# A hint for ScalarE's branch, one output store on ScalarE's queue, and a fallback path whose transfers go to GpSimd's queue

## The chip, the core and the metric

The kernel runs on one core of a Trainium2 chip. A core has TensorE (matrix multiplications, PE in the profile, with its weight loads as PEld), VectorE (DVE), ScalarE (ACT), GpSimd (POOL) and SyncE (SP, which here only issues transfers). Each engine works through its own list of instructions; they wait for each other and for transfers on semaphores. The metric is the device time of one execution in microseconds; the time of a kernel is the median of several runs.

## What is computed

Two parts follow each other. The first is an attention over blocks: a small matrix P of 8 x 8 per batch and head is normalised five times by rows and columns (Sinkhorn), the blocks of k and v are mixed by P, and each of the 8 blocks of 96 queries attends to its own mixed block. The second is a gated layer with a spatial mixing over the 768 positions.

```python
P = sort_net                                # (4, 8, 8, 8)
for _ in range(5):
    P = exp(P - max(P, -1)); P = P / (sum(P, -1) + 1e-9); P = P / (sum(P, -2) + 1e-9)
k_sorted, v_sorted = P @ blocks(k), P @ blocks(v)
attn = softmax(scale * q_b @ k_sb.T)        # per block of 96
x = (attn @ v_sb) as (4, 768, 512)
h = relu(x @ w_in); u, v = halves of h      # 512 + 512
v_n = (v - mean) / sqrt(var + 1e-6)
gated = u * (w_spatial @ v_n + b_spatial)
out = gated @ w_out                         # (4, 768, 512), float32
```

## The kernel before

Inputs of the four batches are loaded in turn and everything stays in on-chip memory until the output. The order of the work is written out by hand in the string ORDER: each word is a unit with its arguments (`OJ:3:4:0:512` calls `u_OJ` for batch 3, tile 4, columns 0 to 512), and each unit appends its instructions to the lists of the engines that it names. Nothing reorders them, so the order of two stores on SP is the order of their words.

Loads of q, k, v and of the weights go through GpSimd's queue (`u_L`, lines 158 to 181). SP issues the first load of sort_net (line 184) and of q (line 343), the copies of mixed v into blocks (`u_VC`, line 418, 24 transfers), four transposing transfers (`u_XD`, line 501), and all stores of the output: `u_OS` (line 645) for two row tiles at once, and for the last batch also `u_OJ` (line 692) for one tile of 128 rows. ScalarE issues no transfer.

The end of the program is batch 3. TensorE multiplies the gated tiles with w_out (`u_OH`, line 680), ScalarE or VectorE copies the result from PSUM to SBUF (`u_OI`, through the helper lines 110 and 112), and SP stores it (`u_OJ`). The last words of ORDER are

```python
OH:1:3:4:0:512:0:4 OI:D:3:0:0:512 OI:D:3:5:256:512 OI:A:3:4:0:512 OJ:3:1:0:512 OJ:3:5:256:512 OJ:3:4:0:512
OJ:3:0:0:512
```

so the last copies are of tile 0 and of half of tile 5 by VectorE and of tile 4 by ScalarE, and the last four stores on SP are those of tile 1, of half of tile 5, of tile 4 and of tile 0.

The fast way through the attention skips the subtraction of maxima. Whether that was safe is found out while the kernel runs: `u_CK` and `u_CF` (lines 694 to 713) form a flag from the sums, and `u_LF` (line 715) loads it into a register on every engine. Behind the last word of ORDER stands an If (line 773): when the flag is above 0, `general_path` (line 724) computes everything again in a safe form. With the inputs given the flag is 0, so the path is skipped: each engine executes a branch over the path's instructions, some semaphore steps on the If's line, and the closing steps on line 800, where SP waits for all semaphores, all engines meet, and the semaphores are cleared.

`u_BH` (line 718) marks the place of a branch hint for TensorE and VectorE; in the trace the two hint instructions stand at 0.8 us, at the start of these engines' lists.

Of the kernel before, what the change touches and what calls it, by code (L numbers as in the profile page):

```python
# [45 lines left out]
SH:3:3:0:0 GH:D:3:0:0 SH:0:3:0:1 OS:2:2 SH:1:3:1:1 GH:P:3:1:1 SH:2:3:3:1 OH:3:3:2:0:512:0:4 GH:D:3:0:1 OS:2:0:0:1  # L46
OS:2:0:1:2 OH:1:3:3:0:512:0:4 GH:P:3:3:1 OI:A:3:2:0:512 OI:A:3:3:0:512 OJ:3:2:0:512 OH:2:3:5:0:256:0:4 OJ:3:3:0:512
OH:0:3:5:256:512:0:4 OI:D:3:5:0:256 OH:3:3:1:0:512:0:4 OH:2:3:0:0:512:0:4 OI:A:3:1:0:512 OJ:3:5:0:256
OH:1:3:4:0:512:0:4 OI:D:3:0:0:512 OI:D:3:5:256:512 OI:A:3:4:0:512 OJ:3:1:0:512 OJ:3:5:256:512 OJ:3:4:0:512
OJ:3:0:0:512  # L50
"""

# [13 lines left out]
def kernel(  # L66
# [12 lines left out]
    nc = tc.nc  # L79

    B, H, S, D = q.shape
# [8 lines left out]
    KC = DM // 128  # L90
    FC = DH // 128
    HP = H // 2
# [11 lines left out]

    def ps_tile(n, dt=FP32):
        return psum.tile([128, 2, 512 if dt == FP32 else 1024], dt, name=f"ps{n}", tag=f"ps{n}")

    def copy(eng, out, in_):
        if eng == "A":
            nc.scalar.copy(out=out, in_=in_)  # L110
        else:
            nc.vector.tensor_copy(out=out, in_=in_)
# [9 lines left out]
    p_all = const.tile([BH, NB, NB], FP32, name="p_all")  # L122
# [27 lines left out]
    st = {}  # L150
# [30 lines left out]
            nc.gpsimd.dma_start(out=w_out_sb, in_=moe_w_out.rearrange("(fc p) n -> p fc n", p=128))  # L181

    def load_sort_net():
        nc.sync.dma_start(out=p_all, in_=sort_net.rearrange("b h i j -> (b h) i j"))

    def u_S0():
        load_sort_net()
# [37 lines left out]
    def u_SK(n, safe=False):  # L225
        n = int(n)
        rows, cols = (first[:, 0:NB], first[:, NB:2 * NB]) if n == 0 else (rowsum, colsum)
        over_rows = lambda x: x.to_broadcast([BH, NB, NB])
        over_cols = lambda x: _raw_ap(x, 0, [x.ap[0], [0, NB], x.ap[1]])
        if safe:  # L230
            nc.vector.reduce_max(out=rowsum, in_=p_all, axis=AX.X)
            nc.vector.tensor_sub(out=p_all, in0=p_all, in1=over_rows(rowsum))
        nc.scalar.activation(out=p_all, in_=p_all, func=AF.Exp)
        nc.vector.reduce_sum(out=rows, in_=p_all, axis=AX.X)
        if safe:
            nc.vector.tensor_scalar_add(out=rows, in0=rows, scalar1=1e-9)
        nc.vector.reciprocal(out=rowsum, in_=rows)
        nc.vector.tensor_mul(out=p_all, in0=p_all, in1=over_rows(rowsum))
        nc.vector.reduce_sum(out=cols, in_=p_all.rearrange("p i j -> p j i"), axis=AX.X)
        if safe:  # L240
            nc.vector.tensor_scalar_add(out=cols, in0=cols, scalar1=1e-9)
        nc.vector.reciprocal(out=colsum, in_=cols)
        to = p16.rearrange("p (i j) -> p i j", i=NB) if n == 4 else p_all
        nc.vector.tensor_mul(out=to, in0=p_all, in1=over_cols(colsum))
        if n == 4:
            nc.vector.transpose(out=p_t, in_=p16)

    def u_PR(ps):
        pr = ps_tile(ps)[:, 0, 0:NB * BH].rearrange("p (i y) -> p i y", i=NB)
        for i in range(NB):  # L250
            nc.tensor.matmul(
                pr[:, i, :], lhsT=spread[:, (i % NI) * NB:(i % NI + 1) * NB].rearrange("p j t -> p (j t)"),
                rhs=p_t[:, (i // NI) * BH:(i // NI + 1) * BH], start=True, stop=True,
            )
        st["pr"] = pr
# [6 lines left out]
    def u_P0(lo, hi):  # L262
        lo, hi = int(lo), int(hi)
        n, pr = hi - lo, st["pr"]
        nc.vector.tensor_mul(
            out=pd(0)[:, lo:hi].rearrange("p h (i t) -> p h i t", t=TB),
            in0=_raw_ap(mask16, 0, [mask16.ap[0], [0, n], [0, NB], [1, TB]]),
            in1=_raw_ap(pr, lo, [pr.ap[0], [1, n], [BH, NB], [0, TB]]),
        )

    def u_PC(eng):
        copy(eng, prep_sb, st["pr"])

    def u_PD(b, lo, hi):
        b, lo, hi = int(b), int(lo), int(hi)
        n = hi - lo
        nc.gpsimd.tensor_mul(
            out=pd(b)[:, lo:hi].rearrange("p h (i t) -> p h i t", t=TB),
            in0=_raw_ap(mask16, 0, [mask16.ap[0], [0, n], [0, NB], [1, TB]]),
            in1=_raw_ap(prep_sb, b * H + lo, [prep_sb.ap[0], [1, n], [BH, NB], [0, TB]]),  # L280
        )
# [103 lines left out]
    def u_KT(ps, eng, b, hp):  # L385
        mixed("k", "kT", ps, eng, int(b), int(hp))
# [14 lines left out]
    def u_VM(ps, eng, b, hp):  # L401
        b, hp = int(b), int(hp)
        t = ps_tile(ps)
        for hh in range(2):
            nc.tensor.matmul(
                t[:, hh, 0:G * D], lhsT=pd(b)[:, 2 * hp + hh, :], rhs=st["v", b][:, 2 * hp + hh, :],
                start=True, stop=True,
            )
        copy(
            eng,  # L410
            vm[:, :, 2 * hp:2 * hp + 2, 0:D].rearrange("p g h d -> p h g d"),
            t[:, :, 0:G * D].rearrange("p h (g d) -> p h g d", g=G),
        )

    def u_VC(b, lo, hi):
        b = int(b)
        for i in range(int(lo), int(hi)):
            nc.sync.dma_start(
                out=vb[b % 2][:, i].rearrange("c h d -> c (h d)"),
                in_=vm[i * TB:(i + 1) * TB].rearrange("t g h d -> t g (h d)"),  # L420
            )
# [75 lines left out]
    def u_XD(b, ih, lo=0, hi=4):  # L497
        b, ih, lo, hi = int(b), int(ih), int(lo), int(hi)
        if ("xT", b) not in st:
            st["xT", b] = att.tile([128, 2, KC, HW], BF16, name="xT", tag="xT", bufs=2)  # L500
        nc.sync.dma_start_transpose(
            out=st["xT", b][:, ih, lo:hi].rearrange("p k (i c) -> p (k i) c", i=NI),
            in_=st["x", b, ih][:, lo:hi].rearrange("p k i c -> p (k i c)"),
        )

    def u_XT(ps, eng, b, ih, lo):
        b, ih, lo = int(b), int(ih), int(lo)
        if ("xT", b) not in st:
            st["xT", b] = att.tile([128, 2, KC, HW], BF16, name="xT", tag="xT", bufs=2)
        t = ps_tile(ps, BF16)[:, 0, 0:2 * HW].rearrange("p (k i c) -> p k i c", k=2, i=NI)  # L510
        for k in range(2):
            for i in range(NI):
                nc.tensor.transpose(t[:, k, i, :], st["x", b, ih][:, lo + k, i, :], ident[0:BLK, 0:BLK])
        copy(eng, st["xT", b][:, ih, lo:lo + 2].rearrange("p k (i c) -> p k i c", i=NI), t)
# [125 lines left out]
            st["o", b, n0] = ld.tile([128, 3, DM], FP32, name="o_sb", tag="ld")[:, 0:2]  # L640
        copy(eng, st["o", b, n0][:, lo:hi], st["o_ps", b, n0][:, lo:hi])

    def u_OS(b, n0, lo=0, hi=2):
        b, n0, lo, hi = int(b), int(n0), int(lo), int(hi)
        nc.sync.dma_start(
            out=out[b].rearrange("(c p) n -> p c n", p=128)[:, n0 + lo:n0 + hi, :],
            in_=st["o", b, n0][:, lo:hi],
        )
# [38 lines left out]
        st["o1", b, n, c0] = ld.tile([128, 3, DM], FP32, name="o1_sb", tag="ld")[:, 0, 0:c1 - c0]  # L687
        copy(eng, st["o1", b, n, c0], st["o1_ps", b, n, c0])

    def u_OJ(b, n, c0, c1):  # L690
        b, n, c0, c1 = (int(x) for x in (b, n, c0, c1))
        nc.sync.dma_start(out=out[b, n * 128:(n + 1) * 128, c0:c1], in_=st["o1", b, n, c0])

    def u_CK():
        nc.vector.memset(bad, 0.0)
# [21 lines left out]

    def u_BH():
        tc.mark_branch_hint_location(
            "general", hint="LikelyTaken", engines=[mybir.EngineType.PE, mybir.EngineType.DVE])  # L720

    units = {name[2:]: f for name, f in locals().items() if name.startswith("u_")}

    def general_path():


        st.clear()
        load_sort_net()
        for n in range(5):
            u_SK(n, safe=True)  # L730
        u_PR(0)
        u_P0(0, 8)
        u_PC("A")
        for b in range(B):
            if b > 0:
                u_PD(b, 0, 8)
            for x in ("q", "k", "v"):
                u_L(x, b, 0, H)
            for hp in range(HP):
                u_VM(2, "A", b, hp)  # L740
            u_VC(b, 0, NB)
            for hp in range(HP):
                u_QN(2, "A", b, hp)
                u_KT(3, "D", b, hp)
                for ih in range(2):
                    u_SM(b, hp, ih)
                    u_AT(2, b, hp, ih)
            for ih in range(2):
                u_XD(b, ih, 0, HP)
            for n in range(0, G, 2):  # L750
                u_VP(n % 4, "A", b, n, n + 1)
                u_ST(b, n)
                u_ST(b, n + 1)
            u_LN(b, 0, G)
            for n in range(G):
                u_LA(b, n)
            for m in range(2):
                for ih in range(2):
                    u_UP(2 * m + ih, "A", b, m, ih)
            for mc in range(FC):  # L760
                u_SP(mc, b, mc)
                u_GT("D", b, mc)
            for n in range(0, G, 2):
                u_OP(n % 4, b, n)
                u_OE("A", b, n)
                u_OS(b, n)
# [38 lines left out]
```

## Time and profile before

| what | value |
|---|---|
| median of 3 runs | 161.39 us (161.30 to 161.57) |
| time of the profiled execution | 161.53 us |
| its span, first to last instruction | 159.7 us |
| granted TensorE clock | 0.996 |
| instructions | 3977 |
| read from HBM / written | 24.78 MB / 6.29 MB |
| line 692 (`u_OJ`), issues on SP | 7, median 333 ns each, 149.8 to 155.4 us |
| line 692, from issue to landing | 2.0 / 2.4 / 2.7 us (lowest, median, highest) |
| GpSimd's last transfer counters on line 773 | 508 ns, at 150.8 us |
| GpSimd's drain on line 800 | 1461 ns, at 151.3 us |

The profile is one execution. A page gives each engine's busy time, the span in 40 slices (a digit is the busy share of the slice in tenths), the transfer queues, the chain of work that ended last, and the costliest groups of instructions. Beside the page there are views of the same trace: the timeline, the instructions of one source line, the waits, and the transfers in a window. A row of a source line has the line, the engine (a q behind its name means its instruction queue: branches, semaphores, transfer issues), the operation, the count, the durations in ns (lowest, median, highest) and the times of the first and last start in us. The time of a run is 1.8 us longer than the span.

### The profile page before, as it was taken

The page shows a single profiled execution, that of the slowest core. Times are in us where ns is not written, and L with a number is a line of the kernel's source. Part 1 is how long each engine was busy: PE and PEld are TensorE (multiplying, and loading weights), DVE is VectorE, ACT ScalarE, POOL GpSimd, SP SyncE. Part 2 cuts the span into 40 slices and gives each one's busy share as a digit, 9 for nine tenths or more (in the row PEclk, how much of TensorE's full clock was granted, in tenths as well). Part 3 has the DMA queues.
Part 4 walks back from the last instruction along what each step waited for, and adds up shares of the span by engine and source line. Part 5 has one row for each costly group of instructions (what it writes and reads, how often), then busy time and mean ns, then how long its engine had stood idle before and what let it go on. Part 6 is the DMA issues. An engine that isn't in the chain of part 4 may idle for free. (4 is left out here: it accounts for less than half of the span.)

```text
span 159.7 us, 3977 instructions
## 1 busy us (share of the span) xinstructions
PE 147.6 (92%) x1647; PEld 89.2 (56%) x1661; DVE 113.1 (71%) x261; ACT 85.7 (54%) x117; POOL 42.2 (26%) x46
## 2 busy tenths in 40 slices
PE   6997989999999999999999999999999999899840
PEld 2355867845686668556465654655655554455410
DVE  4786889638995679867838669897558956947620
ACT  3556799968889409478572446555432242340220
POOL 7942782292000034040000650210004440005300
PEclk9999999999999999999999999999999999999998
DMA  3999999999999999950000657300911377037253
GB/s 84 259 204 204 204 208 202 208 224 239 269 207 202 204 226 241 214 92 4 0 4 0 123 90 131 61 4 0 290 71 34 69 259 266 0 137 259 96 202 112
DMA packets 27526, 23.58 MB, mean 148 GB/s; under 512 B 7280, under 2 KB 24432, under 8 KB 27504
## 3 DMA queue, kind: packets, MB, share of 16 engines
q0 software_dynamic: 14352, 11.80, 46.6%
q1 hardware_dynamic: 13152, 11.49, 25.1%
q8 instruction: 14, 0.23, 0.6%
q14 instruction: 8, 0.07, 0.2%
HBM read 24.78 MB, written 6.29 MB: 195 GB/s over the span
## 5 line engine op out<-in xcount | busy, mean ns | idle before, releaser
L620 POOL TENSOR_TENSOR gt<-z,u_sb 128x768 bf16<-128x768 f32 x10 | 16.4, 1642 | 76.1 <-DVE rec_all L490 55.1
L442 ACT ACTIVATE ex<-ps 96x768 bf16<-96x768 f32 x32 | 24.4, 804 | 7.9 <-PE ps L437 7.8
L604 PE MATMUL ps<-wspT,v_sb 128*128 128x384 bf16 x144 | 25.4, 326 | 0.0
L592 PE MATMUL ps<-xT,w_in_sb 128*128 128x384 bf16 x128 | 23.3, 326 | 0.6 <-ACT o_sb L110 0.6
L491 DVE TENSOR_TENSOR x_sb<-ps,rec_all 96x512 bf16<-96x512 f32 x32 | 22.0, 687 | 1.1
L549 PE MATMUL ps<-w_in_sb,xT 128*128 128x512 bf16 x88 | 21.6, 379 | 0.5 <-issue 0.2
L566 DVE BATCH_NORM_STATS2 stats<-v_sb 128x6 f32<-128x512 bf16 x24 | 16.3, 680 | 5.5 <-ACT v_sb L116 4.3
L610 DVE TENSOR_TENSOR z<-ps,b_bc 128x768 f32<-128x768 f32 x12 | 11.5, 956 | 11.2 <-PE ps L604 11.2
L604 PEld LDWEIGHTS <-v_sb 128*128 128x128 bf16 x144 | 13.3, 98 | 8.4
L116 ACT ACTIVATE u_sb<-ps 128x768 bf16<-128x768 f32 x15 | 12.2, 812 | 10.8 <-PE ps L592 7.9
L116 ACT ACTIVATE v_sb<-ps 128x1024 bf16<-128x1024 f32 (+1 forms) x10 | 9.8, 982 | 14.4 <-PE ps L549 14.4
L592 PEld LDWEIGHTS <-w_in_sb 128*128 128x128 bf16 x128 | 11.8, 98 | 8.7 <-issue 0.9
L630 PE MATMUL ps<-w_out_sb,gt 128*128 128x512 bf16 x68 | 16.3, 379 | 0.2
L110 ACT COPY o_sb<-ps 128x1024 f32<-128x1024 f32 (+1 forms) x10 | 8.4, 839 | 14.7 <-PE ps L680 10.6
L549 PEld LDWEIGHTS <-xT 128*128 128x128 bf16 x96 | 8.9, 98 | 9.8
L483 PEld LDWEIGHTS <-ex 96*128 96x128 bf16 x256 | 10.9, 97 | 3.8 <-DVE x_sb L491 0.3
L483 PE MATMUL ps<-vb,ex 96*128 96x65 bf16 x256 | 12.4, 193 | 0.1
L110 ACT CAST kt<-ps 128x768 bf16<-128x768 f32 x12 | 9.3, 804 | 5.9 <-PE ps L378 5.9
L221 PE MATMUL ps<-warm 128*128 128x512 bf16 x35 | 10.0, 441 | 1.3 <-DVE warm L194 1.3
L630 PEld LDWEIGHTS <-gt 128*128 128x128 bf16 x72 | 6.6, 98 | 7.1
L437 PE MATMUL ps<-qT,kt 64*128 64x96 bf16 x256 | 9.3, 204 | 0.5 <-DVE x_sb L491 0.2
L490 DVE RECIPROCAL rec_all<-ps 96x8 f32<-96x8 f32 x32 | 6.3, 197 | 4.8 <-PE ps L483 4.4
(94 smaller groups left out, 198.5 us busy)
## 6 DMA issues: line engine op xcount, KB each, us to landing
out_dram<-o_sb SPq DMA_DIRECT2D x8, 512.0 KB, 3.7
k_in<-in_k_dram POOLq DMA_DIRECT2D x4, 768.0 KB, 23.9
v_in<-in_v_dram POOLq DMA_DIRECT2D x4, 768.0 KB, 22.8
vb<-vm SPq DMA_DIRECT2D x24, 99.0 KB, 5.6
q_in<-in_q_dram POOLq DMA_DIRECT2D x3, 768.0 KB, 29.0
out_dram<-o_sb SPq DMA_DIRECT2D x7, 256.0 KB, 2.6
ws_in<-in_moe_w_spatial_dram POOLq DMA_DIRECT2D x2, 576.0 KB, 27.8
w_in_sb<-in_moe_w_in_dram POOLq DMA_DIRECT2D x2, 512.0 KB, 23.9
```

The costliest lines, as they stand in the source:

```text
L110: nc.scalar.copy(out=out, in_=in_)
L116: nc.scalar.activation(out=out, in_=in_, func=AF.Relu)
L442: nc.scalar.activation(out=e_tile(b, hp, ih).rearrange("p h (x g) -> p h x g", g=G), in_=t[0:BLK, :, 0:HW].rearrange("p h (g x) -> p h x g ...
L483: nc.tensor.matmul(t[:, hh, ii * VW:ii * VW + D + 1], lhsT=e[:, c:c + 128], rhs=vb[b % 2][:, ih * NI + ii, 2 * hp + hh, 0:D + 1], start=Tr ...
L491: nc.vector.tensor_mul(out=x_sb[:, hp].rearrange("p i (h d) -> p h i d", h=2), in0=tv[:, :, :, 0:D], in1=_raw_ap(rec, 0, [rec.ap[0], [NI, ...
L549: nc.tensor.matmul(t[:, x, :], lhsT=st["xT", b][:, n // 3, kc, (n % 3) * 128:(n % 3 + 1) * 128], rhs=w_in_sb[:, kc, DH:DFF], start=(kc == ...
L566: nc.vector.bn_stats(out=stats, in_=st["v_sb", b, n])
L592: nc.tensor.matmul(t[:, x, 0:HW], lhsT=w_in_sb[:, kc, mc * 128:(mc + 1) * 128], rhs=st["xT", b][:, ih, kc, :], start=(kc == 0), stop=(kc = ...
L604: nc.tensor.matmul(t[:, x, 0:HW], lhsT=st["v_sb", b, n][:, mc * 128:(mc + 1) * 128], rhs=wspT[:, 3 * x:3 * x + 3, n, :], start=(n == 0), s ...
L610: nc.vector.tensor_add(out=z.rearrange("p (x c) -> p x c", x=2), in0=t[:, :, 0:HW], in1=b_bc.rearrange("p (x c) -> p x c", x=2),)
L620: eng.tensor_mul(out=gt, in0=st["z", b, mc], in1=st["u", b, mc // 2][:, mc % 2])
L630: nc.tensor.matmul(t[:, x, :], lhsT=st["gt", b, mc][:, (n0 + x) * 128:(n0 + x + 1) * 128], rhs=w_out_sb[:, mc, :], start=(mc == 0), stop=( ...
```

## The change

Four edits, all in the text below.

1. The hint names ScalarE too.
2. `u_OJ` and `u_OS` get an argument for the engine that issues, and the store of tile 4 of batch 3 names ScalarE ("A"). On SP's list it is gone; on ScalarE's it stands behind the copy of that tile, ahead of the branch.
3. A helper `queue` picks the engine that issues. While `general_path` is being written out, `st["general"]` is set, and then it is always GpSimd: the transfers of `load_sort_net`, `u_VC` and `u_OS` in that path leave SP.
4. In that path the four times two transposing transfers of `u_XD` are replaced by `u_XT`: per call 8 transposes on TensorE into PSUM and one copy by ScalarE, two calls in place of each transfer.

```diff
-OH:1:3:4:0:512:0:4 OI:D:3:0:0:512 OI:D:3:5:256:512 OI:A:3:4:0:512 OJ:3:1:0:512 OJ:3:5:256:512 OJ:3:4:0:512
+OH:1:3:4:0:512:0:4 OI:D:3:0:0:512 OI:D:3:5:256:512 OI:A:3:4:0:512 OJ:3:1:0:512 OJ:3:5:256:512 OJ:3:4:0:512:A
 OJ:3:0:0:512
...
+    def queue(eng):
+        if "general" in st:
+            return nc.gpsimd
+        return nc.scalar if eng == "A" else nc.sync
...
     def load_sort_net():
-        nc.sync.dma_start(out=p_all, in_=sort_net.rearrange("b h i j -> (b h) i j"))
+        queue("S").dma_start(out=p_all, in_=sort_net.rearrange("b h i j -> (b h) i j"))
...
     def u_VC(b, lo, hi):
-            nc.sync.dma_start(
+            queue("S").dma_start(
...
-    def u_OS(b, n0, lo=0, hi=2):
+    def u_OS(b, n0, lo=0, hi=2, eng="S"):
-        nc.sync.dma_start(
+        queue(eng).dma_start(
...
-    def u_OJ(b, n, c0, c1):
+    def u_OJ(b, n, c0, c1, eng="S"):
-        nc.sync.dma_start(out=out[b, n * 128:(n + 1) * 128, c0:c1], in_=st["o1", b, n, c0])
+        queue(eng).dma_start(out=out[b, n * 128:(n + 1) * 128, c0:c1], in_=st["o1", b, n, c0])
...
     def u_BH():
         tc.mark_branch_hint_location(
-            "general", hint="LikelyTaken", engines=[mybir.EngineType.PE, mybir.EngineType.DVE])
+            "general", hint="LikelyTaken", engines=[mybir.EngineType.PE, mybir.EngineType.DVE, mybir.EngineType.Activation])
...
     def general_path():
         st.clear()
+        st["general"] = True
         load_sort_net()
...
             for ih in range(2):
-                u_XD(b, ih, 0, HP)
+                for lo in range(0, KC, 2):
+                    u_XT(2 + lo // 2, "A", b, ih, lo)
```

## The prediction

> **What bounds the kernel now.** I read the page first, then the chain of work that ended last, then the stretch after the last arithmetic, line by line.
>
> ```profile
> PE 147.6 (92%) x1647; PEld 89.2 (56%) x1661; DVE 113.1 (71%) x261; ACT 85.7 (54%) x117; POOL 42.2 (26%) x46
> PE   6997989999999999999999999999999999899840
> DMA  3999999999999999950000657300911377037253
> ```
>
> TensorE bounds the body, up to 153.7 us. In the last slice, and most of the one before it, TensorE is idle and only transfers and bookkeeping are left. Every part of the change that is executed lies there, except a hint of some 50 ns. So I price the tail alone. The chain gives the point where arithmetic ends (start us, us, what):
>
> ```profile
> 150.36 3.32 PE ps L680 x17
> 153.68 0.03 ACTq L110
> 153.71 0.04 issue
> 153.75 0.59 ACT o_sb L110
> ```
>
> ScalarE's last copy, of the tile that the change lets ScalarE store, ends at 154.34. The span ends at 159.7: 5.4 us of tail. The timeline of SP, in narrow windows, shows the last two stores:
>
> ```profile
> 154.36 0.62 SPq L692 DMA_DIRECT2D out_dram<-o_sb  x1
> ```
> ```profile
> 155.43 0.33 SPq L692 DMA_DIRECT2D out_dram<-o_sb  x1
> ```
>
> The first of them stores ScalarE's tile and starts 0.02 us after the copy. The second stores a tile that VectorE had ready at about 153.4: it only stands behind the first in SP's queue. Its landing takes 2.5 us (view of line 692 for that instruction), so it lands at about 157.95. Then the branch line (773) and the end (800):
>
> ```profile
> L773 SPq EVENT_SEMAPHORE  x8: 17/17/17, 156.0 to 158.0; - x8
> ...
> L773 POOLq INC_SWDGE_SEM  x1: 508/508/508, 150.8 to 150.8; - x1
> ...
> L773 DVEq COMPARE_BRANCH  x1: 84/84/84, 153.0 to 153.0; - x1
> ...
> L773 ACTq COMPARE_BRANCH  x1: 50/50/50, 153.8 to 153.8; - x1
> L773 DVEq EVENT_SEMAPHORE  x1: 21/21/21, 153.9 to 153.9; - x1
> L773 SPq COMPARE_BRANCH  x1: 58/58/58, 155.8 to 155.8; - x1
> L773 ACTq EVENT_SEMAPHORE  x1: 17/17/17, 156.6 to 156.6; - x1
> ```
> ```profile
> L800 SPq EVENT_SEMAPHORE  x12: 28/28/28, 158.0 to 158.7; - x12
> L800 SPq DRAIN  x1: 13/13/13, 158.8 to 158.8; - x1
> ```
>
> Three things are to be seen. (1) SP executes eight semaphore steps on the If's line, spread from 156.0 to 158.0, and the last stands right behind the landing. I read them as bookkeeping: a path that is not taken would have issued transfers on SP, and SP waits for each of its eight transfer semaphores and adds what that path would have added. (2) Only then do SP's twelve final waits run, all long satisfied, from 158.02 to 158.77: 0.062 us each, in series, behind the last landing. From the first SP drain to the end it is 159.74 - 158.77 = 0.97 us. (3) ScalarE, without a hint, stands still for 2.8 us between its branch (153.8) and its next instruction (156.6). VectorE, with a hint, needs at most 0.9 us, and it was still busy with its last copy until 153.86.
>
> **Part A: the general path's transfers leave SP.** By the code, the skipped path has 53 transfers on SP (1 sort_net, 32 of u_VC, 8 transposes, 12 stores) and 12 on GpSimd. Afterwards SP has none and GpSimd 57; the 8 transposes become 16 ScalarE copies and 128 TensorE transposes, all in the path that is skipped. With nothing to make up for, SP's eight steps should go. Then the final waits run while the stores are still under way, and behind the last landing only the wait for that semaphore and at most one more remain: 0.08 to 0.14 us instead of 158.77 - 157.94 = 0.83. Saved: 0.69 to 0.75, taken as **0.70**. The cover is the flight of the last store, some 2.5 us, against eleven waits of 0.68 us. GpSimd's bookkeeping (0.51 us from 150.8) and the drain behind it (1.46 us from 151.3) are over at 152.8, long before SP's end. Whether their price grows with the transfers skipped, no row shows; bounds: nothing, and 57/12 = 4.75 times (the slower rival). I take nothing, since it is one instruction for all of them.
>
> **Part B: ScalarE issues the store.** What stands behind the new instruction on ScalarE is only its branch. SP loses the 154.36 store, so the 155.43 one moves up behind SP's previous store, which is issued at 153.89 and takes 0.34: it starts at about 154.27, 1.16 earlier. ScalarE's store starts at about 154.36, as now. No row shows a store issued by ScalarE. Bounds for the issue: 0.33 us (SP's undisturbed stores) and 0.93 us (GpSimd's slowest issue of q_in at the start); I take SP's row, since form and size are the same. Now the landing is bound by bytes: two stores of 256 KB nearly at once. Bytes start some 0.8 us after an issue (slices of the transfers: 155.43 is followed by bytes from 156.2), so from 155.1. The rate of back-to-back stores:
>
> ```profile
> 142.40:146.20 3.80, 3.80 (x23) 2.13 (x22) 2.19 (x4) 0.00 (x0) 2.10 (x2) 1.00 1.02 379
> ```
>
> The last column is GB/s: 524 KB / 379 = 1.38 us, so the bytes are through at 156.5. From that point, reckoned in the same way, to the last landing the two undisturbed stores at 149.76 and 150.62 need 0.53 to 0.57 us, the last two 0.88 and 1.05. So the landing is at 157.03 to 157.55; I take 157.25, between the bounds. Saved: 157.95 - 157.25 = **0.70** (0.40 to 0.92).
>
> At this place the Trainium skill speaks against the change (DMA: Bandwidth & Descriptors, Issuing engines are not separate DMA queues): transfers started by several engines share the same 16 DMA engines, and one gains only the time of issuing. The trace agrees so far that the last store's own bytes ran at about the rate of the earlier ones; by the rule alone Part B would be worth one issue, which is a rival below.
>
> **Part C: the hint on ScalarE.** One more instruction at the start; the two hints now there take 50 and 51 ns at 0.8 us. ScalarE's table load (0.75 to 2.04) is followed by 0.37 us of idle time until the sort_net transfer has landed, so it costs nothing; without that cover it would cost 0.05. Its gain now is nothing by itself, since ScalarE is ready at 156.7 and SP at 158.8. It matters with Part B: ScalarE's branch moves behind its store, to about 154.75. With the hint (VectorE's row, at most 0.9 us) ScalarE is through by 155.7, before SP's 157.4; without it, 157.6. There is a second tie: SP's 154.36 issue took 0.62 instead of 0.33, and the next began 0.45 us after its end where 0.05 is usual. Two instruction fetches stand in the transfer view at that time (154.4 and 154.7). Two of SP's u_VC issues that overlap a fetch took 1.44 and 1.30 us instead of 0.6. So ScalarE's missed branch seems to have delayed the last store by up to 0.7 us; that lies inside the 1.16 of Part B and is not counted twice.
>
> **Sum.** 0.70 + 0.70 = 1.40 us. The profiled execution has a span of 159.74 and a time of 161.53; the span goes to 158.34 and the time to 160.13. The median shown, 161.39, is 0.14 below that execution, so I forecast 161.39 - 1.40 = **160.0**.
>
> **Rivals.**
> - R1, the bookkeeping stays: SP keeps its eight steps, because they are not what I take them for. For it: nothing shows a kernel without them. Against it: they stand on the If's line and wait for exactly SP's own transfers (1.7 us in three waits). Only B is left: 161.39 - 0.70 = 160.7.
> - R2, the two stores get in each other's way, or ScalarE's issue is slow. B is then one issue, 0.33 us: 161.39 - 0.33 - 0.70 = 160.4. With ScalarE's issue at 0.93, its bytes start 0.6 later, B falls to about 0.1, and the time is 160.6. For it: the bytes are already the longest piece of the new tail. Against it: in the old tail the transfer engines had a gap before the 154.36 store's bytes.
> - R3, the hint doesn't work on ScalarE: branch at 154.75, 2.8 us as now, ready at 157.6 and 0.25 behind SP. Gain 1.15 to 1.2: 160.2. Against it: VectorE's row. In the Trainium skill (Runtime: NRT & Kernel Launch, Instruction fetch mechanics) a taken branch to a page outside the two that are held has to fetch it; ScalarE's 2.8 us beside SP's 0.14 agrees.
> - R4, slower: GpSimd's bookkeeping grows with the number of transfers that it makes up for. GpSimd now spends 0.51 + 1.46 = 1.97 us from 150.76 on, and may spend 6.5 before it ends later than SP's new 157.3: it decides from 3.3 times. At 4.75 times it is 9.4 us, to 160.1; the closing steps behind SP's drain, 0.87, follow: span 161.0, time 162.7. For it: both rows are far longer than any other semaphore step. Against it: the instruction is one, and its drain is no count.
>
> **Chances.** Forecast 0.58; R1 0.11; R2 0.13, of which 0.03 within 0.2%; R3 0.06; R4 0.07; what I have not seen 0.05 (0.02 no change, 0.03 slower). About 0.2% is what a measurement of this kernel can tell from no change. Faster 0.58 + 0.11 + 0.10 + 0.06 = 0.85; the same 0.05; slower 0.10. The forecast's own bounds are 1.09 to 1.67 us of gain, 159.7 to 160.3. The range takes in R1, R2 and R3, and half a measurement's spread (0.14) below and above: 159.5 to 160.9.
>
> **What would show it.** A: no SP steps on the If's line, and at most two final waits of SP behind the last landing. B: one store on ScalarE at about 154.4, SP's last at about 154.3, and a last landing near 157.25. C: ScalarE's next instruction less than a microsecond behind its branch. R4: GpSimd's increment over 0.51 us or its drain over 1.46. The prediction is wrong if the body moves at all, that is, if ScalarE's last copy doesn't end within some 0.2 us of 154.3, or if the last landing stays near 157.9.

## The result, and the profile after

| kernel | median us | runs | against the kernel before, 95% interval |
|---|---|---|---|
| before | 161.34 (161.26 to 161.57) | 6 | |
| changed | 159.94 (159.85 to 160.09) | 6 | 0.9911 (0.9899 to 0.9922) |

The change makes the kernel 1.40 us faster; 160.0 was forecast. The profiled execution has a time of 159.85 and a span of 158.1.

The page of the changed kernel, its slices and its transfer queues (packets, MB, share of 16 engines):

```profile
PE   6898999999999999999999999999999999899880
...
DMA  3999999999999999970000557500840549009064
...
q1 hardware_dynamic: 13008, 11.23, 25.0%
...
q10 hardware_dynamic: 144, 0.26, 0.4%
```

There is a new queue, q10: it holds ScalarE's one store. TensorE is busy for 8 tenths of slice 39, for 4 before: the span behind it has become shorter. The chain still ends in the same copy, and the timeline shows it with the two stores behind it (start us, us):

```profile
153.48 0.59 ACT o_sb L115
```
```profile
154.02 0.71 SPq L697 DMA_DIRECT2D out_dram<-o_sb  x1
154.10 0.38 ACTq L697 DMA_DIRECT2D out_dram<-o_sb  x1
```

ScalarE's last copy ends at 154.07, against 154.33 before. Over all kernels below that keep the If and VectorE's hint this point lies between 154.01 and 154.33 (the kernel before itself at the upper end, the others up to 154.18), so I take its shift for the scatter of single executions and not for a gain. The times say the same: the profiled execution of before was 0.19 above its median, that of the changed kernel 0.09 below. From here on I count from the end of this copy, since every part of the change that matters lies behind it or within 0.1 us of it. SP's last store is now issued 0.05 us ahead of that point; before it was 1.10 behind. A store reports its landing on a semaphore in 16 parts, and its landing is the time of the last part. SP's last store took 3.1 us from issue to landing (line 697, this instruction alone; 2.5 before):

```profile
DMA to landing us min/median/max: 3.1/3.1/3.1
```

The If's line (780 now) and SP's final waits (line 807), the rows that answer to those of before:

```profile
L780 POOLq INC_SWDGE_SEM  x1: 508/508/508, 150.5 to 150.5; - x1
...
L780 ACTq COMPARE_BRANCH  x1: 68/68/68, 154.5 to 154.5; - x1
L780 SPq COMPARE_BRANCH  x1: 54/54/54, 154.8 to 154.8; - x1
L780 ACTq EVENT_SEMAPHORE  x1: 17/17/17, 155.0 to 155.0; - x1
```
```profile
L807 SPq EVENT_SEMAPHORE  x12: 28/28/28, 155.3 to 157.1; - x12
L807 SPq DRAIN  x2: 7/10/13, 157.2 to 157.2; - x2
```

SP has no row of semaphore steps on the If's line any more. Its twelve final waits begin at 155.3, while the stores are still under way, and end at 157.1 with the last landing. ScalarE goes on 0.5 us behind its branch. GpSimd's increment takes the same 508 ns for 57 transfers as for 12, and its drain the same 1461.

| from the end of ScalarE's last copy, us | before | after | saved | forecast |
|---|---|---|---|---|
| last store's issue | 1.10 | -0.05 | 1.15 | 1.16 |
| last landing | 3.61 | 3.01 | 0.59 | 0.70 |
| from the last landing to the end | 1.80 | 0.98 | 0.82 | 0.70 |
| end of the span | 5.40 | 3.99 | 1.41 | 1.40 |

### The profile page after: what moved, and what is told of

Same layout as the page of the kernel before. It is cut to its first block, busy times and chain, and to the rows that moved or that the text cites. A ratio compares the mean times of both kernels' runs of the same rounds, so it can differ in the third digit from the quotient of the medians.

```text
span 158.1 us, 3983 instructions
## 1 busy us (share of the span) xinstructions
PE 148.6 (94%) x1661; PEld 89.1 (56%) x1661; DVE 113.0 (72%) x261; ACT 85.8 (54%) x117; POOL 42.2 (27%) x46
## 5 line engine op out<-in xcount | busy, mean ns | idle before, releaser
L554 PE MATMUL ps<-w_in_sb,xT 128*128 128x512 bf16 x96 | 22.6, 379 | 0.0
```

Of the source, the lines that this page charges most:

```text
L554: nc.tensor.matmul(t[:, x, :], lhsT=st["xT", b][:, n // 3, kc, (n % 3) * 128:(n % 3 + 1) * 128], rhs=w_in_sb[:, kc, DH:DFF], start=(kc == ...
```

## The experiments

The three executed parts of the change are A (the general path's transfers leave SP), B (ScalarE stores tile 4) and C (ScalarE's hint). All eight combinations were run; the medians stand against the kernel before in the same comparison. An interval reaches 0.15 to 0.25 us to either side, so a difference between two rows is uncertain by 0.2 to 0.3 us. Edits are shown against the changed kernel where nothing else is said, and of a line of ORDER or of the hint only the piece that changes.

| parts | median us | against before, us | ratio, 95% interval |
|---|---|---|---|
| A | 160.39 | -0.92 | 0.9946 (0.9933 to 0.9959) |
| B | 161.16 | -0.15 | 0.9989 (0.9980 to 0.9999) |
| C | 161.17 | -0.14 | 0.9994 (0.9986 to 1.0003) |
| A, B | 160.91 | -0.40 | 0.9977 (0.9967 to 0.9986) |
| A, C | 160.36 | -0.90 | 0.9939 (0.9923 to 0.9954) |
| B, C | 160.66 | -0.60 | 0.9951 (0.9937 to 0.9966) |
| A, B, C | 159.94 | -1.40 | 0.9911 (0.9899 to 0.9922) |

### A alone

```diff
-OJ:3:4:0:512:A
+OJ:3:4:0:512
-engines=[mybir.EngineType.PE, mybir.EngineType.DVE, mybir.EngineType.Activation]
+engines=[mybir.EngineType.PE, mybir.EngineType.DVE]
```

> Only the general path's transfers go to GpSimd (and its transposes to TensorE); SP stores tile 4 again and ScalarE has no hint. Theory: SP's eight steps on the If's line are gone, and behind the last landing one or two final waits are left. The stretch from the last landing to the end shrinks from 1.80 to about 0.98 us, the stretch from ScalarE's last copy to the last landing stays near 3.6: time 161.34 - 0.82 = 160.5. Rival (the shorter closing came from the store's move and not from this edit): the eight steps stay and the time is 161.3.

Measured: 160.39. SP's steps on the If's line are gone; its final waits begin at 155.5, ahead of the landing (the row has the twelve waits and two closing steps):

```profile
L807 SPq EVENT_SEMAPHORE  x14: 17/28/28, 155.5 to 158.5; - x14
```

The last landing is 3.52 us behind the copy (3.61 before) and the end 0.97 behind the landing (1.80). Part A does what it was priced for, by itself.

### B alone

The hint as in the kernel before, and `general_path` with its SP transfers and `u_XD` again:

```diff
-        st["general"] = True
...
-                for lo in range(0, KC, 2):
-                    u_XT(2 + lo // 2, "A", b, ih, lo)
+                u_XD(b, ih, 0, HP)
```

> Only the store of tile 4 goes to ScalarE; the general path keeps SP, ScalarE has no hint. Theory: from ScalarE's last copy to the last landing 3.0 us in place of 3.6, from there to the end 1.80 as before: 161.34 - 0.6 = 160.75. Rival (the two stores share the transfer engines, so that only one issue of 0.33 us is won): 161.0. Rival (ScalarE without a hint delays its own or SP's store by a fetch): 161.3 or more.

Measured: 161.16, between the two rivals and for neither's reason. The last landing is where the theory has it, 3.07 us behind the copy. But SP is no longer the last engine: ScalarE is. Line 778 of this kernel:

```profile
L778 ACTq COMPARE_BRANCH  x1: 54/54/54, 154.6 to 154.6; - x1
...
L778 ACTq EVENT_SEMAPHORE  x1: 17/17/17, 158.2 to 158.2; - x1
```

From its branch to its next instruction ScalarE now needs 3.6 us, not the 2.8 of the kernel before, and SP's wait for ScalarE's semaphore ends there.

### C alone

Only the hint, everything else as before.

> Only the hint on ScalarE; store and general path as before. Theory (ScalarE's missed branch fetches code while SP issues its last two stores and holds them up): the fetch at 154.7 is gone, the gap of 0.45 us ahead of SP's last store falls to 0.05, and the last landing comes 0.3 to 0.7 us earlier: 160.65 to 161.05. Rival (the hold-up comes from another fetch, the one behind VectorE's branch, or from no fetch): issue 0.62 us and gap 0.45 as before, time 161.3.

Measured: 161.17; the interval takes in no change. ScalarE's next instruction, and SP's last two issues (the copy ends at 154.03):

```profile
L778 ACTq EVENT_SEMAPHORE  x1: 17/17/17, 154.1 to 154.1; - x1
```
```profile
154.23 0.37 SPq L697 DMA_DIRECT2D out_dram<-o_sb  x1
```
```profile
155.06 0.33 SPq L697 DMA_DIRECT2D out_dram<-o_sb  x1
```

ScalarE goes on as soon as its copy has ended, so the hint does its work, but SP's last store is issued 1.03 us behind the copy (1.10 before), and the gap of 0.45 us ahead of it is there as before. The theory that ScalarE's missed branch makes this gap has failed. A fetch as such is not yet ruled out: one still moves; it begins at 154.55, inside the issue of 0.37, and runs into the gap behind it. The merged store below decides that.

### A and B without C

> The changed kernel without the hint on ScalarE. Theory: ScalarE's branch stands behind its store, its next instruction comes 2.8 us later, 3.2 to 3.3 us after its last copy, where SP is ready at 3.17: the end moves by 0.05 to 0.2 us, time 160.0 to 160.15. Rival (the fetch holds up the stores' bytes): last landing later than 3.2 us after the copy and a time of 160.4 or more. Rival (the hint is worth nothing): 159.94.

Measured: 160.91; against the kernel before it gains 0.40 us, 1.00 less than with the hint. The price of a missing hint was put at 0.05 to 0.2. The branch line of this kernel, and its transfers (q14 holds code fetches, q1 and q10 the stores) from 154.6 to 156.5 and from 156.5 to 157.0:

```profile
L780 ACTq COMPARE_BRANCH  x1: 54/54/54, 154.6 to 154.6; - x1
L780 ACTq EVENT_SEMAPHORE  x1: 17/17/17, 158.2 to 158.2; - x1
```
```profile
q1 hardware_dynamic: 262, 0.37, 54.9%
q10 hardware_dynamic: 144, 0.26, 37.1%
```
```profile
q14 instruction: 2, 0.02, 7.7%
q1 hardware_dynamic: 8, 0.00, 3.6%
```

No code is fetched while the two stores' bytes move; two fetches stand right behind them, at 156.65 and 156.68, 2.1 us behind the branch. In the kernel before, the branch came ahead of these bytes, and a fetch moved at 154.7, 0.9 behind it (its transfers from 154.6 to 156.0):

```profile
q14 instruction: 1, 0.01, 3.0%
```

In all five kernels in which ScalarE's branch has no hint, its next instruction starts 1.2 to 1.3 us behind the end of this fetch (of the later one, where there are two). The changed kernel has the same two fetches, at 156.59 and 156.61, but with the hint ScalarE is on by 155.0 and doesn't wait for them. Wherever ScalarE issues a store, no fetch moves while this store's bytes do, and the next stands at their end: 2.4 to 2.6 us behind the copy in most kernels, 1.9 to 2.0 in the two below whose bytes end earlier. It is not a rule for every fetch: in A alone one moves at 156.04, in the middle of the last store's bytes (156.0 to 156.3), so why it waits here is open. So ScalarE, which had 2.1 us to spare before (156.7 against SP's 158.8), becomes the last engine twice over: its branch now stands behind its store, and its fetch behind the bytes of both stores. Its next instruction comes 4.06 us behind the copy, where SP would have been done at 3.1 to 3.2. The same lateness stands in B alone, where it costs 0.26 us between the profiles of B and of B and C; their medians are 0.50 apart, so about half of that difference is seen. In the profile of A and B one part of SP's store landed at 3.67, later than in the changed kernel, but ScalarE was later still.

### A and C, and B and C

> The changed kernel with tile 4 stored by SP again: general path on GpSimd and ScalarE's hint remain. Theory: last landing 3.5 us behind the copy as in the kernel with the general path alone, and the hint adds nothing: 160.4; the store is then worth 0.45 us when the hint is there. Rival (the hint also frees SP's issue): 160.0 to 160.2.

Measured: 160.36, as the theory says. The hint adds nothing to A. The store is worth 0.50 us on top of A and C (1.40 - 0.90); its profile agrees, with a last landing at 3.50 in place of 3.01.

> The store of tile 4 on ScalarE with ScalarE's hint, the general path as before. Theory: without a missed branch ScalarE is ready 0.9 us behind its copy, the last landing comes 3.0 us behind the copy, and SP's twelve waits follow it: 161.3 - 0.6 = 160.7. Rival (the parts help only together): 161.1 or more.

Measured: 160.66. Landing 3.06 us behind the copy, the end 1.71 behind that. With the hint, B gives 0.60, where 0.70 was taken (0.40 to 0.92).

### One transfer less on SP, in the kernel before

```diff
-OH:3:3:2:0:512:0:4 GH:D:3:0:1 OS:2:0:0:1
-OS:2:0:1:2 OH:1:3:3:0:512:0:4
+OH:3:3:2:0:512:0:4 GH:D:3:0:1 OS:2:0
+OH:1:3:3:0:512:0:4
```

> The kernel before with two stores of batch 2 (tiles 0 and 1, one after the other in the order) merged into one, so that SP's list is one transfer shorter. Theory: the 0.45 us ahead of SP's last store belong to a place in SP's list (ahead of its 80th instruction in each trace so far); the place now falls behind the last store, the gap is 0.05, the last landing comes 0.3 to 0.4 us earlier, and the time is 160.9 to 161.0. Rival (the gap belongs to this store, which follows the one ahead of it without a semaphore step, or to a fetch): gap 0.45 as before, time 161.3.

Measured: 161.08, ratio 0.9986 (0.9975 to 0.9996). SP's last two issues in this kernel (the timeline), and its branch:

```profile
154.12 0.64 SPq L692 DMA_DIRECT2D out_dram<-o_sb  x1
```
```profile
154.80 0.61 SPq L692 DMA_DIRECT2D out_dram<-o_sb  x1
```
```profile
L773 SPq COMPARE_BRANCH  x1: 58/58/58, 155.9 to 155.9; - x1
```

The second store follows the first at once (154.76 to 154.80). The gap of 0.45 us now stands behind it, ahead of the branch (155.41 to 155.86), which is now the 80th instruction that SP executes; before, the 80th was the last store. In the changed kernel the 80th is the first instruction behind the branch, and it starts 0.47 us behind the branch where 0.14 was usual. In all fourteen traces of this case 0.45 to 0.47 us pass between the 79th instruction that SP executes and the 80th, whether the 80th is a store, a branch or a wait, and in nine of them, this one included, no fetch moves at that time. So the gap belongs to a place in SP's list. The last landing comes at 3.31 in place of 3.61, with both issues at 0.6 us in this execution. By the medians the gain is 0.18, less than the 0.3 to 0.4 expected.

### VectorE without its hint

> The changed kernel without the hint on VectorE (TensorE and ScalarE keep theirs). SP's last issue took 0.71 us in the changed kernel, beside ScalarE's issue (0.03 to 0.41 us behind the copy) and a fetch (0.09 to 0.41). Theory F (a fetch behind VectorE's branch slows the issue): VectorE's fetch now comes at about 0.5 us ahead of the copy's end, SP's issue at -0.44 takes 0.5 or more and the last one about 0.35 to 0.4. Theory S (two issues at once slow each other): the last one stays at 0.6 to 0.7. VectorE itself is late by 2 to 3 us and still ready before SP: time within 0.3 us of 159.9.

Measured: 160.41. SP's last issue stays at 0.62 us, the one ahead of it at 0.34. But the fetch that the experiment was to move hardly moved: it stands 0.03 us ahead of the copy's end, in place of 0.09 behind it. The two theories are not told apart. VectorE goes on 3.2 us behind its branch, so its hint works too. The last landing is 3.25 and the copy ends 0.2 to 0.5 us later than in the other kernels; it gains only 0.77 us against the kernel before, 0.63 less than the changed kernel. Between the two profiled executions the later copy (0.47) and the later landing (0.23) make up the whole 0.71; why they are later is open.

### Without the If

```diff
-        with tc.If(st["beyond"] > 0, preferred_fallthrough_block=True, label="general"):
-            general_path()
```

The word that marks the hints (`BH`) goes too.

> The changed kernel with the If, its path and the hints left out: the fallback for unsafe inputs is missing, the rest is the same. No branch, so no code is fetched behind one. Theory F: SP's last issue takes 0.33 to 0.39 us, ScalarE's 0.38. Theory S: SP's last issue still 0.6 to 0.7. Bytes theory (the last landing is set by 640 KB at 380 GB/s from the first issue on, not by the issue's length): last landing 2.9 to 3.05 us behind the copy in both. The closing from the last landing stays 0.98 us; time 159.6 to 159.9.

Measured: 159.62, ratio 0.9906 (0.9889 to 0.9922). SP's last issue, beside ScalarE's:

```profile
153.11 0.43 SPq L697 DMA_DIRECT2D out_dram<-o_sb  x1
```
```profile
153.21 0.37 ACTq L697 DMA_DIRECT2D out_dram<-o_sb  x1
```

Without a fetch behind a branch the issue takes 0.43 in place of 0.71 us. So most of the lengthening goes with the If, and up to 0.1 is left for the two issues at once. That it is the If's fetches is likely and not shown: in A alone two issues beside fetches took 0.34 and 0.33. The last landing is 3.12 us behind the copy; the end is 1.53 behind it, not 0.98: two waits in place of one stand behind the landing, GpSimd stands still for 0.43 us in place of 0.07 ahead of its closing drain, and this drain takes 244 ns in place of 107. The copy ends 0.9 us earlier, at 153.18: the other four engines no longer load the flag into a register, which takes 0.5 us on TensorE and GpSimd and 1.1 to 1.2 on ScalarE and VectorE, but whether that is the whole reason was not tried.

### SP's last two stores swapped

```diff
-OJ:3:1:0:512 OJ:3:5:256:512 OJ:3:4:0:512:A
-OJ:3:0:0:512
+OJ:3:1:0:512 OJ:3:0:0:512 OJ:3:5:256:512 OJ:3:4:0:512:A
```

> The changed kernel with SP's last two stores in the order in which their tiles are ready: tile 0 (ready 1.08 us ahead of ScalarE's last copy's end) ahead of half of tile 5 (0.47 ahead). Theory: SP issues nothing at the time of ScalarE's store, ScalarE's 256 KB are the only bytes left at the end, and the last landing comes 2.2 to 2.6 us behind the copy in place of 3.01: 159.94 - 0.4 to 0.8 = 159.15 to 159.55. Rival (the flight of the last store is fixed, whatever lies beside it, or ScalarE's first store of the program is slow): last landing at 2.9 or later, 159.8 to 160.0.

Measured: 159.78, ratio 0.9899 (0.9881 to 0.9916); it can't be told from the changed kernel's 0.9911. Tile 0 is ready 0.80 us ahead of the point, not 1.08 (its copy and the next one overlap in the merged row that I read; the 153.4 of the prediction has the same slip, it is 153.53, and nothing in the sum hangs on it). SP's two issues:

```profile
153.34 0.67 SPq L696 DMA_DIRECT2D out_dram<-o_sb  x1
```
```profile
154.11 0.58 SPq L696 DMA_DIRECT2D out_dram<-o_sb  x1
```

The first takes 0.67 us beside the fetch behind TensorE's branch, so the second is pushed to the time of ScalarE's, and its 128 KB land last, at 2.90. The expected 2.2 to 2.6 has failed; the landing is the rival's, though not for its reason, since ScalarE's own store has landed at 2.40.

> As the one without the If (the fallback is left out), with SP's last two stores swapped, tile 0 first. In the swap with the If, SP's issue of tile 0 took 0.67 us beside the fetch behind TensorE's branch, and its bytes began 0.3 us late. Theory F: that issue now takes 0.33, bytes begin at about 0.0 from the copy's end instead of 0.35, and the last landing comes 2.4 to 2.6 us behind the copy. Rival (the issue is slow because of the stores already under way): 0.6 again and a landing at 2.9.

Measured: 159.75, ratio 0.9909 (0.9892 to 0.9925). Both issues are short again:

```profile
152.66 0.34 SPq L696 DMA_DIRECT2D out_dram<-o_sb  x1
```
```profile
153.10 0.37 SPq L696 DMA_DIRECT2D out_dram<-o_sb  x1
```

The bytes begin at about 0.0 and are through at 1.9. Of the 16 parts of ScalarE's store 15 have landed at 2.39, as the theory says, and the last at 3.06: the landing as a whole is not earlier. The transfers suggest what this part waits for. A fetch begins at 155.33 and takes 0.31 us, and two last packets of the store stand behind it, at 155.64 and 155.72 (the transfers from 155.4 to 155.9, in slices of 0.0125 us):

```profile
DMA  0000000000000000004000000600000000100000
```

The packets carry no name of a transfer engine, so that they wait for this fetch on one of the 16 is a reading of the times. A late part of that kind stands in most of these tails. In the kernel before, the store issued at 152.59 has 15 of 16 parts at 0.25 and the last at 0.99 us behind the copy's end, after the fetch behind TensorE's branch; without the If that store's last part is at 0.25.

### Half of tile 5 earlier

```diff
-OI:A:3:1:0:512 OJ:3:5:0:256
+OI:A:3:5:256:512 OI:A:3:1:0:512 OJ:3:5:0:256 OJ:3:5:256:512
...
-OI:D:3:0:0:512 OI:D:3:5:256:512 OI:A:3:4:0:512 OJ:3:1:0:512 OJ:3:5:256:512 OJ:3:4:0:512:A
+OI:D:3:0:0:512 OI:A:3:4:0:512 OJ:3:1:0:512 OJ:3:4:0:512:A
```

> The changed kernel with the second half of tile 5 copied by ScalarE ahead of tile 1 (ScalarE is idle there for 1.4 us) in place of VectorE behind tile 0, and stored ahead of tile 1. Its 128 KB then move in the hole ahead of the tail, and 512 KB are left at the end, the first 256 KB of them issued about 0.8 us ahead of ScalarE's last copy's end. Bytes theory: last landing 2.3 to 2.6 us behind the copy in place of 3.01, time 159.94 - 0.4 to 0.7 = 159.25 to 159.55. Rival (a single part that a code fetch holds up sets the last landing whatever the bytes): 2.9 or later, 159.8 to 159.95.

Measured: 160.12, ratio 0.9921 (0.9907 to 0.9935): no gain. The transfers of the changed kernel and of this one, in 40 slices of the 3.03 us from 154.07 and of the 3.5 us from 154.0 (a digit is the busy share in tenths):

```profile
DMA  0300049999626999999999999899995305000000
```
```profile
DMA  3000004999999999999998702000000000000000
```

The bytes are through at about 156.0 here, against 156.4, and 13 parts of ScalarE's store have landed at 2.45. The other three come at 2.72, 2.77 and 3.14. The landing is the rival's: fewer bytes at the end do not bring it forward. Its reason fits too, by the times: of the two fetches at the end of the bytes the first is over at 156.31, when the last but one of the data packets of ScalarE's store begins, and the last is through at 156.53, against 156.60 in the changed kernel.

## Why the prediction was right, and where it was not

**What bounds the tail** was right. ScalarE's last copy ended 0.26 us earlier, slightly more than the 0.2 that the prediction allowed before it would call itself wrong, but as said above this shift is scatter as far as these traces tell. The stretch behind it became 1.41 us shorter between the two profiled executions, and the median fell by 1.40. That the sum comes out so close is in part luck: A was taken 0.12 too small and B 0.11 too large.

**Part A** was right in mechanism and somewhat small: 0.70 was taken, 0.82 measured. One wait is left behind the last landing, as supposed (0.08 us from landing to drain); the rest is the closing steps from SP's first drain on, which the forecast carried over as 0.97 and which took 0.90. That the eight steps on the If's line belong to the skipped transfers is shown by A alone: the transfers leave SP, the steps go.

**Part B** came out at 0.59, for 0.70 taken and bounds of 0.40 to 0.92. The issue moved by 1.15 (1.16 forecast). The bytes of the two stores moved without a hole from about 155.0 to 156.4, where the working has 155.1 to 156.5; the 128 KB of the store ahead were through at 154.85, and a dip of 0.1 us lies between. But the reason given, that bytes set the landing, holds only in part. The kernels that begin or end the bytes earlier land at 2.90 to 3.14 all the same, by late parts. The estimate of 2.92 us behind the copy came within 0.1 of the landing (3.01), in part by luck: a landing set by the bytes alone was not what these kernels have.

**Part C** costs nothing, as forecast: ScalarE's first activation starts at 2.42, for 2.41 before. Its reasoning failed twice, without harm to the forecast since the hint works. Its price, 0.2 us if it were missing (rival R3), is 1.00: the 2.8 us were carried over from a branch that stood ahead of the stores' bytes to one that stands behind two stores' issues. And the second tie, that ScalarE's missed branch had delayed SP's last store by up to 0.7 us, is refuted by C alone and the merged store: 0.41 of it belongs to a place in SP's list, and the long issue of 0.62 came and went with and without ScalarE's fetch (0.34 in A alone, 0.56 in A and C).

**The rivals.** R1 (the steps stay): refuted. R2 (the stores get in each other's way): partly so, SP's issue takes 0.58 to 0.71 us beside ScalarE's when there is an If, but B is still worth 0.50 with A and C. The Trainium skill (DMA: Bandwidth & Descriptors, Issuing engines are not separate DMA queues) would give one issue. That is 0.33 by SP's undisturbed rows, but the issue that leaves SP took 0.56 in A and C, and the measured 0.50 lies between, so this case does not speak against the page. It doesn't show that the issue is all of it, either: the last store also no longer stands behind the 0.41 us of its 80th place, and its own issue has become longer. R4 (GpSimd's bookkeeping grows): refuted, 508 and 1461 ns in both kernels.

**Left open.** Why an issue in the tail takes 0.33 us or 0.54 to 0.77: it is long only beside a fetch or another engine's issue, but in A alone two issues beside fetches took 0.34 and 0.33. Which fetch holds up which part of a store, but for the two traces above: landings and packets carry no name of a transfer engine. No version here is faster than the changed kernel beyond the intervals.

## What to carry to other kernels

Behind the last arithmetic, read the tail instruction by instruction: semaphore steps that wait for the last store and are followed by more waits in series cost their full length, and a path that is never taken can put them there. A branch that is off the chain that ends last stays off it only as long as nothing is put ahead of it; when a store moves to another engine, reckon that engine's branch anew, with its fetch behind the store's bytes, as it stood in every such kernel here. Price parts together as well as alone: here the store without its hint took back 0.52 us of what the first part had won, and with it added 0.50.

## What was not expected of the hardware

- A taken branch without a hint took 2.8 us to the next instruction when its fetch moved 0.9 us behind it, and 3.6 when the bytes of two stores of 256 KB lay ahead and the fetch moved 2.1 us behind it; with the hint 0.5 (all on ScalarE).
- SP stood still for 0.41 us more than usual ahead of its 80th executed instruction, in every trace; with a merged store it moved with the count and not with the store. The Trainium skill (Runtime: NRT & Kernel Launch, Instruction fetch mechanics) has instructions come in blocks and calls the step over a block's end mostly hidden. A place fixed by count would suit the end of a block, but no row shows where a block ends, so that this is such a step is not shown; what is shown is that these 0.41 us are not hidden.
- One or a few of the 16 parts of a store landed 0.3 to 1.8 us behind the others (0.25 against 0.99 us for the store issued at 152.59 before, 0.25 for all parts without the If).
